# An attention and expert kernel: W1's transfers, the window copies, the early passes and the one-hots, re-cut

## The chip, the core and the metric

The kernel runs on one core of a Trainium2 chip. The metric is device time in microseconds of one execution; a median of three runs is given. PE is TensorE, DVE VectorE, ACT ScalarE, POOL GpSimd, SP SyncE, which here only issues transfers.

## What is computed

```python
# q, k, v: [8, 8, 576, 64] (batch, head, token, channel)
q_s = softmax(q, axis=-1); k_s = softmax(k, axis=2)
kv = einsum('bhsd,bhse->bhde', k_s, v)
x = einsum('bhsd,bhde->bhse', q_s, kv)         # as [4608, 512]
logits = x @ w_gate + modality_bias[modality_id]   # 8 experts
e_idx = argmax(logits); gate_w = softmax(logits)[e_idx]
for e in range(8):                              # w1 [512, 1024], w2 [1024, 512]
    out[mask] = gate_w * (relu(x[mask] @ w1[e]) @ w2[e])
```

There are two modalities. Each one's largest bias names the expert that the kernel assumes for its tokens; at the end it counts on the chip whether that held, and a loop (from line 1074) computes all experts if not.

## The kernel before, in words

Tokens are sorted by modality as they come out of the attention. `xs` holds 4,864 slots of x, transposed: tokens of modality a are filled in from the left, those of b from the right. For each batch, `attention(b)`:

- ACT takes the exponentials of q and k; DVE sums q's (line 642), and DVE or POOL multiplies by the inverse (`norm_q`, line 651, one instruction of 2,304 columns per batch). V is cast to bf16.
- PE forms kv (line 713), multiplies q by a 0/1 matrix that sorts each tile of 64 tokens (`perm`, made by nine comparisons in `perm_run`, line 675; PE line 780), ACT or DVE evicts (line 789), PE multiplies by kv (line 818).
- `put` (line 837) copies each of the nine tiles twice, to a's and to b's place: ACT writes a's, DVE writes b's. The place is a register; each batch loads nine of them on each of the two engines (`load_off`, line 758). A copy is 64 slots wide, and its last part may hold tokens of the other side, which the next copy of the same side overwrites; so copies of one side are chained.

`ffn` (line 952) runs passes over slots, `passes_a` and `passes_b` (line 203): start and width of the slots, and the batch after which they are full. In a pass PE computes 8 groups of h (line 934), ACT or DVE applies relu (lines 908, 910), PE computes y per 128 slots (line 944), the result is scaled by the gate (lines 914, 916), and POOL stores rows to their tokens by an indirect DMA (line 919). Before the first pass PE must have found which token stands in which slot: one-hots `hlo` and `hhi`, `hv` = `hhi` times the token numbers on POOL, and 36 matmuls (`id_run`, line 572). `hlo` lies in W's second half, so the second expert's casts wait for `id_run`.

The weights of the two experts come in eight tiles (`load_w`, line 414) through the same five fp32 buffers `st` as q, k and v, and are cast into `W`. A W1 tile is two transfers of 128 partitions whose pattern in DRAM is two blocks of 64 rows:

```python
ap=[[2 * Dh * F, 2], [F, Dh], [1, F]]
```

All of this is handed to a planner (`Plan.order`, line 83) as operations with costs per engine, dependencies, buffers and ranks. It plays them through and writes the program in the order in which it started them; transfers keep the order in which they were declared: q, k, v of batches 0 and 1, both experts' weights, then batches 2 to 7. On the chip each engine executes its list strictly in order.

## Time and profile before

| | |
|---|---|
| runs | 327.39 us median (327.07 to 327.65) |
| profiled execution | 328.85 us, span 327.1 us |
| busy in the span | PE 187.6, DVE 185.7, POOL 107.6, ACT 107.1 us |
| moved | 46.57 MB, 142 GB/s over the span |
| granted clock of PE | 0.893 mean |

Busy shares are averages over stages with different limits; they say little before the span is cut. Register and sequencer work is not in them. A wait is put down to what ended last.

### The profile page before, as it was taken

Reading aid. Unit: us, or ns where it says so; the run is one execution under the profiler, and the core shown is the slowest. Engines: PE = TensorE matmul, PEld = TensorE weight load, DVE = VectorE, ACT = ScalarE, POOL = GpSimd, SP = SyncE. Lnnn points to the kernel's source line nnn. Section 1 sums busy time; section 2 is a strip of 40 time slices with the busy share of each in tenths; the row PEclk is TensorE's granted clock in tenths of the full one; section 3 lists DMA queues with packets and bytes.
Section 4 is the critical chain, followed back from the end, with each engine's and each line's share of the span. In section 5 each row is a group of like instructions: output and inputs, shape, how many; then the busy total and the mean of one; then the engine's idle time right before and its main releaser. Section 6 shows DMA issues by size and latency. Waiting matters only on the chain. (4 is left out here: it accounts for less than half of the span.)

```text
span 327.1 us, 4307 instructions
## 1 busy us (share of the span) xinstructions
PE 187.6 (57%) x1450; PEld 107.1 (33%) x1471; DVE 185.7 (57%) x411; ACT 107.1 (33%) x192; POOL 107.6 (33%) x113
## 2 busy tenths in 40 slices
PE   0024400038600007679758966549879999999960
PEld 0023300026400005356424534225544444445520
DVE  1799670001700037649789959795776647567530
ACT  3227210035311017348696865525641000000000
POOL 5449000127100013536972629042201331413330
PEclk9999999999955555989979999598989999999995
DMA  7592114511114599897666981000200211202110
GB/s 257 162 395 110 54 53 125 188 52 51 55 53 150 171 362 308 282 355 262 256 213 206 395 325 64 2 0 34 97 3 24 105 65 65 116 33 111 57 54 25
DMA packets 20731, 46.57 MB, mean 142 GB/s; under 512 B 3039, under 2 KB 3039, under 8 KB 20704
## 3 DMA queue, kind: packets, MB, share of 16 engines
q1 hardware_dynamic: 15888, 36.70, 32.2%
q0 software_dynamic: 3040, 9.44, 7.4%
q10 hardware_dynamic: 1776, 0.10, 0.4%
q8 instruction: 13, 0.21, 0.3%
q14 instruction: 14, 0.11, 0.1%
HBM read 36.80 MB, written 9.96 MB: 143 GB/s over the span
## 5 line engine op out<-in xcount | busy, mean ns | idle before, releaser
L934 PE MATMUL ff<-xs,W 128*128 128x512 bf16 (+2 forms) x376 | 82.3, 371 | 43.6 <-ACT W L451 19.9
L944 PE MATMUL ff<-W,hT 128*128 128x512 bf16 x291 | 69.4, 386 | 1.1 <-issue 0.2
L919 POOL DMA_INDIRECT out_dram<-y_sb,idx x38 | 37.7, 992 | 95.9 <-DVE y_sb L916 67.6
L934 PEld LDWEIGHTS <-W 128*128 128x128 bf16 x384 | 39.7, 107 | 76.0 <-ACT W L451 21.8
L845 DVE CAST xs<-mm 128x256 f32 x72 | 30.6, 424 | 45.5 <-ACT xs L845 41.7
L944 PEld LDWEIGHTS <-hT 128*128 128x128 bf16 x304 | 29.5, 99 | 33.8 <-issue 1.9
L916 DVE TENSOR_SCALAR y_sb<-ff,gate 128x512 f32<-128x512 f32 x30 | 22.5, 749 | 26.4 <-PE ff L944 22.9
L910 DVE TENSOR_SCALAR hT<-ff 128x512 bf16<-128x512 f32 (+2 forms) x54 | 32.5, 605 | 7.7 <-PE ff L934 6.0
L845 ACT CAST xs<-mm 128x256 f32 (+1 forms) x72 | 27.3, 379 | 21.1 <-DVE xs L845 17.4
L453 POOL CAST W<-st 128x1024 bf16<-128x1024 f32 x7 | 7.3, 1040 | 78.5 <-DMA st<-in_moe_w_dram 39.1
L451 ACT CAST W<-st 128x1024 bf16<-128x1024 f32 x8 | 8.4, 1044 | 69.1 <-DMA st<-in_moe_w_dram 69.1
L652 POOL TENSOR_TENSOR eq<-st,qi 128x2304 bf16<-128x2304 f32 x5 | 20.2, 4048 | 21.7 <-DVE L L889 9.2
L678 POOL TENSOR_SCALAR perm<-iota_row,posx 128x128 bf16<-128x128 bf16 x36 | 23.3, 662 | 8.0 <-DVE posx L504 7.3
L878 PE MATMUL mm<-wg_sb,xs 128*128 128x8 bf16 x152 | 5.5, 168 | 31.2 <-DVE L L889 28.5
L818 PE MATMUL mm<-et,kvbd 128*128 128x128 bf16 (+1 forms) x160 | 14.3, 226 | 15.6 <-DVE xs L845 11.0
L639 ACT ACTIVATE st<-st 128x2304 f32<-128x2304 f32 x8 | 17.0, 2124 | 18.9 <-DMA st<-in_q_dram 16.8
L908 ACT ACTIVATE hT<-ff 128x256 bf16<-128x256 f32 (+1 forms) x42 | 19.3, 482 | 10.3 <-PE ff L934 6.0
L713 PE MATMUL kv<-vb,ek 64*128 64x129 bf16 x288 | 13.0, 246 | 16.8 <-DVE vb L668 16.4
L642 DVE TENSOR_REDUCE qi<-st 128x36 f32<-128x2304 f32 x8 | 20.3, 2542 | 2.4 <-issue 2.2
L780 PE MATMUL mm<-perm,eq 128*128 128x128 bf16 x144 | 14.5, 239 | 8.6 <-DVE eq L652 3.0
L818 PEld LDWEIGHTS <-kvbd 128*128 128x128 bf16 x160 | 11.4, 104 | 20.3 <-issue 16.7
L660 ACT ACTIVATE ek<-st 128x2304 bf16<-128x2304 f32 x8 | 17.0, 2122 | 2.4 <-DMA st<-in_k_dram 2.4
(106 smaller groups left out, 166.6 us busy)
## 6 DMA issues: line engine op xcount, KB each, us to landing
st<-in_q_dram SPq DMA_DIRECT2D x8, 1152.0 KB, 8.7
st<-in_k_dram SPq DMA_DIRECT2D x8, 1152.0 KB, 11.2
st<-in_v_dram SPq DMA_DIRECT2D x8, 1152.0 KB, 11.6
st<-in_moe_w_dram SPq DMA_DIRECT2D x16, 512.0 KB, 18.1
out_dram<-y_sb,idx POOLq DMA_INDIRECT x38, 2.7
mraw<-in_moe_modality_id_dram ACTq DMA_DIRECT2D x2, 36.0 KB, 8.6
wg_f<-in_moe_w_gate_dram ACTq DMA_DIRECT2D x4, 4.0 KB, 2.9
bias_b<-n_moe_modality_bias_dram ACTq DMA_DIRECT2D x1, 8.0 KB, 8.1
```

What stands on the lines that cost most here:

```text
L639: nc.scalar.activation(out=t, in_=t, func=ACT.Exp)
L642: nc.vector.tensor_reduce(out=small[qib.idx], in_=view(st[bq.idx], [[Dh, HG * NJ], [1, Dh]]), op=ALU.add, axis=AX.X)
L652: (nc.vector if e == "DVE" else nc.gpsimd).tensor_tensor(out=view(eq[eqb.idx], [[Dh, HG], [HG * Dh, NJ], [1, Dh]]), in0=view(st[bq.idx], [ ...
L678: (nc.vector if e == "DVE" else nc.gpsimd).tensor_scalar(out=perm[pmb.idx][:, j, :], in0=iota_row, scalar1=posx[:, c : c + 1], scalar2=Non ...
L818: nc.tensor.matmul(out=view(mm_t[xbuf.idx], [[1, nj * 64]], c * nj * 64), lhsT=kvbd[kvb.idx][:, c, :], rhs=et[etb.idx][:, c, j0 * 64 : (j0 ...
L845: w_ = nc.scalar.copy(out=dst, in_=src) if side == 0 else nc.vector.tensor_copy(out=dst, in_=src)
L908: nc.scalar.activation(out=dst, in_=src, func=ACT.Relu)
L910: nc.vector.tensor_scalar_max(out=dst, in0=src, scalar1=0.0)
L916: nc.vector.tensor_scalar(out=dst, in0=src, scalar1=g, scalar2=None, op0=ALU.mult)
L919: s_ = nc.gpsimd.indirect_dma_start(out=out, out_offset=bass.IndirectOffsetOnAxis(ap=ix[:, c : c + 1], axis=0), in_=ysb, in_offset=None, b ...
L934: nc.tensor.matmul(out=t[:, 0:w], lhsT=W[:, slot_, kd * F + f * P : kd * F + (f + 1) * P], rhs=xs[:, kd, lo : lo + w], start=(kd == 0), st ...
L944: nc.tensor.matmul(out=t, lhsT=h[:, kf, i * P : (i + 1) * P], rhs=W[:, slot_, W2 + kf * D : W2 + (kf + 1) * D], start=(kf == 0), stop=(kf ...
```

## The change

- W1: a tile comes as two transfers of 64 partitions, 2 x 1,024 values each, so that 64 rows are the outermost dimension on both sides. W2: a tile is one transfer instead of two. (The loop for all experts, which these inputs do not enter, is cut alike.)
- Window copies: both copies of a tile go to one engine, fixed per batch (`copier`): ACT in six batches, DVE in batches 2 and 5. That engine alone loads the offsets, nine instead of eighteen; b's place is computed from a's. Each copy is now made to follow the one two before it.
- Passes: per side 256, 256, 256, 256, 512, 512, 384 slots instead of 256, 256, 512, 512, 512, 384; slots 512 to 1,023 are due after batches 2 and 3 instead of 3.
- One-hots: `hlo` lies in the middle of `xs`, which no copy reaches before batch 3. The second expert's casts no longer wait for `id_run`; the clearing of the middle does, and so comes later. `hv` is made in six pieces. Offsets and the numbers compared are bf16.
- `norm_q` in five pieces; `perm` in one instruction on DVE, no longer on POOL. Ranks of casts and of the slot work are lower, that is earlier.

```diff
-    passes_a = [(0, 0, 256), (1, 256, 256), (3, 512, 512), (5, 1024, 512), (7, 1536, 512), (7, 2048, 384)]
+    passes_a = [(0, 0, 256), (1, 256, 256), (2, 512, 256), (3, 768, 256), (5, 1024, 512), (7, 1536, 512), (7, 2048, 384)]
...
-    hlo = view(W[:, 1, :], [[P, HC], [1, P]])
+    def hlo(c, n):
+        a = CAP - HC // 8 * P + (c % (HC // 4)) * P
+        return xs[:, c // (HC // 4), a : a + n * P].rearrange("p (c m) -> p c m", m=P) if n > 1 else xs[
+            :, c // (HC // 4), a : a + P
+        ]
...
+                if part < 2:
+                    for g in range(2):
                         nc.sync.dma_start(
-                            out=st[buf.idx][:, c * F : (c + 1) * F],
+                            out=view(t, [[F, 2], [1, F]], 0, (64 * g, 64)),
                             in_=bass.AP(
                                 tensor=moe_w1.tensor,
-                                offset=eids[eid] * (D * F) + (4 * hp + hl) * Dh * F,
-                                ap=[[2 * Dh * F, 2], [F, Dh], [1, F]],
+                                offset=eids[eid] * (D * F) + (2 * g + part) * Dh * F,
+                                ap=[[F, Dh], [4 * Dh * F, 2], [1, F]],
                             ),
                         )
...
-                deps = [ld] + ([o_id] if s == 1 else [])
                 casts.append(
                     pl.op(
-                        {**on_act(F), **on_dve(F, 2), **on_pool(F, 1.05)}, cast, deps, rank=40 + s, uses=[buf]
+                        {**on_act(F), **on_dve(F, 2), **on_pool(F, 1.05)}, cast, [ld], rank=5 + 10 * s, uses=[buf]
...
-    o_hv = pl.op(on_pool(HC * NSL * 2, 2.85), hv_run, [o_hhi], rank=30)
+    o_hv = [pl.op(on_pool(HC * NSL // 3, 2.57), hv_run(i), [o_hhi], rank=16) for i in range(6)]
+    c_mid = pl.op({"POOL": (1.9, 2.1)}, clear_mid, [o_id], rank=25)
...
+    copier = ["ACT", "ACT", "DVE", "ACT", "ACT", "DVE", "ACT", "ACT"]
...
-        def perm_run(e):
-            for j in range(NJ):
-                c = b * NJ + j
-                (nc.vector if e == "DVE" else nc.gpsimd).tensor_scalar(
-                    out=perm[pmb.idx][:, j, :],
-                    in0=iota_row,
-                    scalar1=posx[:, c : c + 1],
-                    scalar2=None,
-                    op0=ALU.is_equal,
-                )
+        def perm_run(_):
+            nc.vector.tensor_tensor(
+                out=perm[pmb.idx],
+                in0=view(iota_row, [[0, NJ], [1, P]]),
+                in1=view(posx, [[1, NJ], [0, P]], b * NJ),
+                op=ALU.is_equal,
+            )
...
-        lo_a = pl.op({"ACT": (0.3, 0.4)}, load_off, [o_off, o_ki], rank=R + 3)
-        lo_b = pl.op({"DVE": (0.3, 0.4)}, load_off, [o_off, o_ki], rank=R + 3)
+        lo = pl.op({copier[b]: (2.0, 2.1)}, load_off, [o_off, o_ki], rank=R + 3)
...
-                        w_ = nc.scalar.copy(out=dst, in_=src) if side == 0 else nc.vector.tensor_copy(out=dst, in_=src)
+                        w_ = nc.scalar.copy(out=dst, in_=src) if e == "ACT" else nc.vector.tensor_copy(out=dst, in_=src)
...
+                    before = win[-2] if len(win) > 1 else filled[b - 1][side - 2] if b else None
                     win.append(
                         pl.op(
-                            on_dve(256) if side else on_act(256),
+                            on_dve(256) if copier[b] == "DVE" else on_act(256),
                             put,
-                            [o3, c_mid, lo_b if side else lo_a],
+                            [o3, c_mid if b >= 3 else None, lo, before],
```

What this makes of the program's order, at three places. First SP's queue, after v of batch 1: the first expert's first tiles. Before (names are `st` buffers and the weights in DRAM; sizes are partitions and the dimensions in one):

```order
L323 DMA st1_64<-in_v_dram 128x4x576
L425 ISA
L425 DMA st2_65<-in_moe_w1_dram 128x1x1024
...
L425 DMA st0_63<-in_moe_w1_dram 128x1x1024
...
L435 DMA st4_67<-in_moe_w2_dram 128x2x512
...
L435 DMA st1_64<-in_moe_w2_dram 128x2x512
```

Now:

```order
L330 DMA st1_64<-in_v_dram 128x4x576
L431 ISA
L431 DMA st2_65<-in_moe_w1_dram 64x2x1024
...
L431 DMA st0_63<-in_moe_w1_dram 64x2x1024
...
L440 DMA st1_64<-in_moe_w2_dram 128x4x512
L440 ISA
L440 DMA st2_65<-in_moe_w2_dram 128x4x512
```

The order of the tiles is kept (each W1 row stands twice, for two transfers); W2's second tile now uses the buffer of W1's first.

Second ACT, from batch 1's last copies to the exponential of batch 2's q. Before (line 845 is a window copy, 451 a cast of W, 639 the exponential):

```order
L845 ISA
L845 COPY xs_61<-mm2_92 128x4x64
L451 CAST W_62<-st2_65 128x1024
L451 CAST W_62<-st0_63 128x1024
L451 CAST W_62<-st4_67 128x1024
L908 ACTIVATE hT1_81<-ff1_94 128x256
L895 ACTIVATE ex_143<-ex_143 128x16 x2
L451 CAST W_62<-st3_66 128x1024
L914 ACTIVATE y_sb0_82<-ff2_95,gate_145 128x512
L914 ACTIVATE y_sb1_83<-ff0_93,gate_145 128x512
L895 ACTIVATE ex_143<-ex_143 128x16 x2
L639 ACTIVATE st1_64<-st1_64 128x2304
```

Now (line 863 is a window copy, 456 a cast of W, 649 the exponential of q, 673 that of k):

```order
L673 ACTIVATE ek1_69<-st4_67 128x4x9x64
...
L456 CAST W_62<-st0_63 128x1024
L810 CAST et1_77<-mm2_92 128x4x128
L780 TENSOR_LOAD off_i_131
L810 CAST et1_77<-mm0_90 128x4x64
L456 CAST W_62<-st3_66 128x1024
L863 ISA
L863 COPY xs_61<-mm2_92 128x4x64
...
L863 COPY xs_61<-mm1_91 128x4x64
L649 ACTIVATE st2_65<-st2_65 128x2304
```

ACT's casts of the second expert's weights moved ahead of batch 1's copies, of which ACT now has 18 instead of 9; the exponential of k of batch 1 moved from ahead of batch 0's copies to behind them and behind relus.

Third PE, at the end of the last batch's attention. Before (line 818 is the last attention matmul, 934 a matmul of h):

```order
L818 MATMUL mm1_91<-et1_77,kvbd1_75 128x64
L934 LDWEIGHTS W_62
L934 MATMUL ff2_95<-xs_61,W_62 128x512
...
L934 MATMUL ff1_94<-xs_61,W_62 128x512
...
L878 LDWEIGHTS xs_61
L878 MATMUL mm2_92<-wg_sb_119,xs_61 128x8
```

Now (line 836 is the last attention matmul, 963 a matmul of y, 897 one of the logits):

```order
L836 MATMUL mm0_90<-et1_77,kvbd1_75 128x64
L963 LDWEIGHTS hT0_80
L963 MATMUL ff0_93<-W_62,hT0_80 128x512
...
L897 LDWEIGHTS xs_61
L897 MATMUL mm2_92<-wg_sb_119,xs_61 128x8
```

The first pass of 512 slots on side a is still in h there before the change, and in y after it.

## Rows read from the trace of the kernel before

**Rows 1.** The page's 40 equal slices: GB/s that DMA moved:

```profile
GB/s 257 162 395 110 54 53 125 188 52 51 55 53 150 171 362 308 282 355 262 256 213 206 395 325 64 2 0 34 97 3 24 105 65 65 116 33 111 57 54 25
```

**Rows 2.** Busy us: PE, PEld, DVE, ACT, POOL; clock, DMA share, GB/s:

```profile
26.00:126.50 100.50, 25.54 (x241) 17.77 (x241) 30.93 (x71) 24.16 (x52) 18.83 (x20) 0.82 0.36 123
126.50:241.50 115.00, 84.82 (x783) 50.89 (x793) 90.39 (x178) 71.07 (x129) 54.43 (x44) 0.91 0.53 188
241.50:316.10 74.60, 74.13 (x385) 35.54 (x393) 46.67 (x94) 2.47 (x7) 20.09 (x21) 0.98 0.17 64
316.10:327.10 11.00, 0.00 (x0) 0.00 (x0) 1.09 (x4) 0.00 (x0) 1.28 (x2) 0.61 0.14 53
```

**Rows 3.** The same view, stretches in which one kind of transfer runs:

```profile
14.00:26.00 12.00, 2.86 (x44) 2.59 (x44) 11.85 (x34) 3.83 (x2) 7.20 (x8) 1.00 1.02 387
28.00:52.00 24.00, 5.25 (x58) 4.01 (x58) 16.59 (x30) 5.98 (x13) 4.02 (x3) 1.00 0.13 53
66.00:100.00 34.00, 15.66 (x150) 10.81 (x152) 7.38 (x19) 11.19 (x25) 9.39 (x13) 0.85 0.13 53
```

**Rows 4.** SP's own queue in order of time: start us, us, what:

```profile
20.09 23.06 SPq L425 DMA_DIRECT2D st<-in_moe_w_dram  x4
...
62.34 29.23 SPq L425 DMA_DIRECT2D st<-in_moe_w_dram  x4
...
110.66 2.93 SPq L323 DMA_DIRECT2D st<-in_q_dram  x1
```

**Rows 5.** Who waited for whom: us in total, times, longest:

```profile
ACT W L451 <- DMA st<-in_moe_w_dram: 69.1, 8, 21.6
```

**Rows 6.** ACT in order of time:

```profile
21.28 2.12 ACT L639 ACTIVATE st<-st 128x2304 f32<-128x2304 f32 x1 [9.17 <-DMA st<-in_q_dram]
...
36.35 1.04 ACT L451 CAST W<-st 128x1024 bf16<-128x1024 f32 x1 [4.46 <-DMA st<-in_moe_w_dram]
...
126.51 2.12 ACT L639 ACTIVATE st<-st 128x2304 f32<-128x2304 f32 x1 [0.56 <-DMA st<-in_q_dram]
```

**Rows 7.** The chain of waits at the end: start us, us, what:

```profile
241.10 0.38 ACT xs L845
...
255.62 6.91 PE ff L934 x32
```

**Rows 8.** DMA issues: KB each, median us to landing:

```profile
st<-in_moe_w_dram SPq DMA_DIRECT2D x16, 512.0 KB, 18.1
```

**Rows 9.** ACT's and DVE's groups by shape: busy, mean ns of one, idle before:

```profile
L845 ACT CAST xs<-mm 128x256 f32 x71 | 26.9, 379 | 20.3 <-DVE xs L845 17.4 <-PE ff L944 1.2 <-PE mm L818 0.6
...
L908 ACT ACTIVATE hT<-ff 128x512 bf16<-128x512 f32 x19 | 10.9, 596 | 2.1 <-PE ff L934 2.0
L908 ACT ACTIVATE hT<-ff 128x256 bf16<-128x256 f32 x23 | 8.4, 388 | 8.2 <-PE ff L934 4.0 <-issue 2.5 <-PE mm L780 1.7
...
L845 DVE CAST xs<-mm 128x256 f32 x72 | 30.6, 424 | 45.5 <-ACT xs L845 41.7 <-PE ff L934 0.4
...
L548 DVE TENSOR_TENSOR W<-iota_row,lo 128x1152 bf16<-128x1152 bf16 x4 | 5.3, 1333 | 0.2 <-issue 0.2
```

**Rows 10.** The offset loads, line 761: ns min/median/max, first and last start:

```profile
L761 ACTq TENSOR_LOAD <-off_i x8: 778/1967/2687, 24.3 to 222.6; - x8
L761 DVEq TENSOR_LOAD <-off_i x8: 853/2082/2742, 25.6 to 222.9; - x8
```

**Rows 11.** POOL's and DVE's rows in order of time, two places:

```profile
170.15 4.05 POOL L652 TENSOR_TENSOR eq<-st,qi 128x2304 bf16<-128x2304 f32 x1 [1.20 <-DVE qi L649]
...
199.69 4.05 POOL L652 TENSOR_TENSOR eq<-st,qi 128x2304 bf16<-128x2304 f32 x1
...
170.83 3.42 DVE L891 TENSOR_TENSOR ex<-L,gmx 128x32 f32<-128x32 f32 x1
...
199.01 7.16 DVE L678 TENSOR_SCALAR perm<-iota_row,posx 128x128 bf16<-128x128 bf16 x9
...
219.25 1.52 DVE L678 TENSOR_SCALAR perm<-iota_row,posx 128x128 bf16<-128x128 bf16 x9
```

More of the change, by code (lines that the diff above doesn't have):

```diff
@@ L317 @@
     c_dve2 = pl.op({"DVE": (0.9, 1.1)}, consts_dve2, [c_pool], rank=-8)
-    c_mid = pl.op({"POOL": (2.3, 2.4)}, clear_mid, [c_pool], rank=-8)
     def load(src, b, buf):
@@ L576, in id_run @@
                 out=view(t, [[NSL, 2], [1, NSL]]),
-                lhsT=hlo[:, c, :],
+                lhsT=hlo(c, 1),
                 rhs=hv[:, c],
@@ L635, in attention @@
         qib, kib, kvp = Buf(r_qi), Buf(r_kinv), Buf(r_kv)
+        groups = [(j0, min(2, NJ - j0)) for j0 in range(0, NJ, 2)]
         def exp_q(_):
@@ L649, in inv_q, with norm_q, run @@
             nc.vector.reciprocal(out=t, in_=t)
-        def norm_q(e):
-            (nc.vector if e == "DVE" else nc.gpsimd).tensor_tensor(
-                out=view(eq[eqb.idx], [[Dh, HG], [HG * Dh, NJ], [1, Dh]]),
-                in0=view(st[bq.idx], [[NJ * Dh, HG], [Dh, NJ], [1, Dh]]),
-                in1=view(small[qib.idx], [[NJ, HG], [1, NJ], [0, Dh]]),
-                op=ALU.mult,
-            )
+        def norm_q(j0, n):
+            def run(e):
+                (nc.vector if e == "DVE" else nc.gpsimd).tensor_tensor(
+                    out=view(eq[eqb.idx], [[HG * Dh, n], [Dh, HG], [1, Dh]], j0 * HG * Dh),
+                    in0=view(st[bq.idx], [[Dh, n], [NJ * Dh, HG], [1, Dh]], j0 * Dh),
+                    in1=view(small[qib.idx], [[1, n], [NJ, HG], [0, Dh]], j0),
+                    op=ALU.mult,
+                )
+            return run
         def exp_k(_):
@@ L692, in attention @@
         iq = pl.op({"DVE": (0.35, 0.5)}, inv_q, [sq], rank=R + 1, uses=[qib])
-        nq = pl.op({**on_dve(S * HG), **(on_pool(S * HG, 2.8) if b > 1 else {})}, norm_q, [iq], rank=R + 1, takes=[eqb], uses=[qib, bq])
+        nq = []
+        for j0, n in groups:
+            n_ = n * HG * Dh
+            nq.append(
+                pl.op(
+                    {**on_dve(n_), **(on_pool(n_, 1.76) if b > 1 else {})},
+                    norm_q(j0, n),
+                    [iq] + nq[:1],
+                    rank=R + 1,
+                    takes=[] if nq else [eqb],
+                    uses=[eqb, qib, bq],
+                )
+            )
         vcost = on_dve(S * 2, 2) if b < 1 else {**on_pool(S * 2, 1.03), **on_dve(S * 2, 2)}
@@ L752, in attention @@
         o_kb = pl.op({"DVE": (0.7, 0.8)}, kvbd_run, [o_ki, c_dve], rank=R + 2, takes=[kvb], uses=[kvp, kib])
-        groups = [(j0, min(2, NJ - j0)) for j0 in range(0, NJ, 2)]
         ets, win, firsts = [], [], []
@@ L758, in load_off @@
         def load_off(e):
-            eng = ENG.Activation if e == "ACT" else ENG.DVE
-            side = 0 if e == "ACT" else 1
             vs = nc.values_load_multi_w_load_instructions(
-                off_i[0:1, side, b * NJ : (b + 1) * NJ],
-                engines=[eng],
+                off_i[0:1, b * NJ : (b + 1) * NJ],
+                engines=[ENG.Activation if e == "ACT" else ENG.DVE],
                 min_val=0,
-                max_val=NSLOT - 64,
+                max_val=N - 64,
                 skip_runtime_bounds_check_because=WHY,
             )[1]
-            av.append((side, vs))
-        lo_a = pl.op({"ACT": (0.3, 0.4)}, load_off, [o_off, o_ki], rank=R + 3)
-        lo_b = pl.op({"DVE": (0.3, 0.4)}, load_off, [o_off, o_ki], rank=R + 3)
+            av.extend(vs)
+        lo = pl.op({copier[b]: (2.0, 2.1)}, load_off, [o_off, o_ki], rank=R + 3)
         for gi, (j0, nj) in enumerate(groups):
@@ L844, in put @@
                         src = view(mm_t[xbuf.idx], [[nj * 64, KD], [1, 64]], jj * 64)
-                        w_ = nc.scalar.copy(out=dst, in_=src) if side == 0 else nc.vector.tensor_copy(out=dst, in_=src)
-                        if not started["ab"[side]]:
+                        w_ = nc.scalar.copy(out=dst, in_=src) if e == "ACT" else nc.vector.tensor_copy(out=dst, in_=src)
+                        if b >= 3 and not started["ab"[side]]:
                             started["ab"[side]] = True
@@ L1099 @@
                 hl, hp = part // 2, part % 2
-                nc.sync.dma_start(
-                    out=t[:, 0:F],
-                    in_=bass.AP(
-                        tensor=moe_w1.tensor,
-                        offset=e * (D * F) + (4 * hp + hl) * Dh * F,
-                        ap=[[2 * Dh * F, 2], [F, Dh], [1, F]],
-                    ),
-                )
+                for g in range(2):
+                    nc.sync.dma_start(
+                        out=t[64 * g : 64 * g + 64, 0:F],
+                        in_=bass.AP(
+                            tensor=moe_w1.tensor,
+                            offset=e * (D * F) + (4 * hp + 2 * g + hl) * Dh * F,
+                            ap=[[F, Dh], [1, F]],
+                        ),
+                    )
             else:
```

83 lines of the change are left out of this document (41 added, 42 removed).

## The prediction

> **What bounds the kernel now.** I read the page's slices first, then the busy time by stage, then DMA alone, then who waits. The slices show the hole: for about 90 us after the first eighth of the span the core moves some 50 GB/s in most slices, with one bump in the middle [rows 1]. By stage the same hole is 26 to 126.5 us: 100.5 us in which no engine is busy for more than 31 us [rows 2]. DMA alone says why. Between 14 and 26 us, when q, k and v arrive, the DMA share is 1.02 at 387 GB/s. In 28 to 52 and again in 66 to 100 us, when the first weight matrix of an expert (W1) arrives, it is 0.13 at 53 GB/s [rows 3]. 0.13 of sixteen engines is two engines, and W1's source pattern begins with a dimension of 2. The queue's own rows fit: each expert's four W1 issues hold SP for 23 and 29 us, so that q of batch 2 is issued only at 110.66 us [rows 4]. ACT waits 69.1 us for weights, more than anything else waits for anything [rows 5].
>
> After that there are two stages. From exp of q2 (126.51 us [rows 6]) to the last window copy (241.1 us to 241.5 [rows 7]) DVE is busy 90.4, PE 84.8 and ACT 71.1 of 115 us [rows 2]. From there only expert matmuls are left, PE is 99% busy for 74.6 us, and the last 11 us store rows and check [rows 2].
>
> So I cost the change in three terms: when q2 is exponentiated, how long the attention stage of batches 2 to 7 takes, what is left after it.
>
> **Term 1, the weights.** The 16 weight issues carry 512 KB each [rows 8], 8.39 MB, half of it W1. At 53 GB/s W1's 4.19 MB take 79 us. In the new form both patterns begin with 64, and half a tile goes to each half of the partitions. The trace has no large transfer with 64 outermost, so I bound it: 53 GB/s (outermost 2) and 387 GB/s (outermost 128) [rows 3]. I take 387: if the share follows the outermost count, 64 is above sixteen. W1 then takes 10.8 us, a saving of 68 us of queue time; all weights and q2 (8 x 576 x 64 values of 4 bytes, 1.18 MB) are 9.57 MB, 24.7 us. First q, k, v are in by 26 us [rows 3], so q2 could land at about 51 us plus the few us from issue to landing. W2's four issues per expert become two of 1 MB; the same bytes in the same queue, costed at nothing, since before they were delayed by W1 ahead of them.
>
> Landing is no longer what is late. ACT executes in program order, and in the new order it has, between exp of q1 at 21.28 us [rows 6] and exp of q2: the two exps (q1, k1) at 2.12, two offset loads at 1.97 [rows 10], 36 window copies at 0.40 (0.379 [rows 9] and the gap between chained copies), 8 evictions of about 0.6, 7 casts of W at 1.04 [rows 6], 8 relus at 0.388 [rows 9], and 1.1 of gates and scaling. That is 4.2 + 3.9 + 14.4 + 4.8 + 7.3 + 3.1 + 1.1 = 39 us, so exp of q2 not before 60 us. The casts wait for tiles whose buffers are freed in turn: W1's second tile needs q0's buffer, W2's second tile needs W1's first tile cast, expert 1's last tile needs k1's exp, which now stands behind casts and relus on ACT. I add 3 us and take **63 us**, with 71 us as the upper end if W1 arrives at half the rate, and 60 us as the lower. Against 126.5 us this is 63.5 us gained.
>
> [...] The trace shows full rate only for transfers that span 128 partitions [rows 3]. [...]
>
> **Term 2, batches 2 to 7.** Costs that leave DVE: 18 window copies of 0.424 (two of the six batches on DVE, where half of each was) = 7.6 us [rows 9]; four of six offset loads of 2.08 = 8.3 us [rows 10], which the busy time does not hold: sequencer time in which DVE stands still. perm becomes one instruction of 1152 columns instead of nine. The kernel has one of that size with two bf16 SBUF inputs, but inside a group with a float offset; I take 1.33 us, that row [rows 9], against 1.52 us for nine when undisturbed and 7.16 us when POOL normalizes q at the same time [rows 11]. Four of them now in this stage: 5.3 against 8.7. Similarly a gate subtraction took 3.42 us while POOL's normalization of 4.05 us ran [rows 11]. POOL's normalization is now in five pieces; if a piece takes its share of 4.05, DVE is held for at most 0.9 us at a time. Over this stage I count 5 us back for it; nothing to 8 are the ends. Costs that come: two more passes of 256 per side in place of one of 512, so 18 more gate instructions of some 0.18 (3.2), four more relus of 256 and three of 512 (3.5, a little over ACT's price [rows 9]); scaling and casts of v that go elsewhere -5. Normalization pieces +1. DVE stood at 90.4 + 6 x 2.08 = 103 of 115 us, 90%. It comes to 103 - 7.6 - 8.3 - 3.4 - 5 + 3.2 + 3.5 - 5 + 1 = 81 us.
>
> ACT takes over. It stood at 71.1 + 6 x 1.97 = 83 us [rows 2, 10]. It gains 18 copies (7.2), loses two loads (3.9), and by the order has 39 relus of 256 and 2 of 512 where it had 14 and 16 (+1.3), four more scalings (2.8), four more gate exps (0.9), one eviction less: 91 us. PE gains some 7 us of expert work, 92 us. So the fullest engines are PE and ACT, and this stage cannot be under 92 us. At the 90% that DVE reached it would be 102; at ACT's present share of 72% it would be 126. Three engines between 75% and 85% full are harder to interleave than one at 90%, so I take **108 us**, 7 less than now.
>
> The one-engine copies make the chain of a batch no shorter: 18 chained copies of 0.40 are 7.3 us on ACT, where they now run partly beside DVE's. hlo in xs in place of W's second half: W's second expert no longer waits for the index matmuls; this is inside term 1. Clearing the middle of xs now waits on POOL for the index matmuls; behind it there stand two casts of expert 1's W2 (1.04 each), which the second pass needs late, and batch 3's copies come tens of us after it: nothing. The product of the one-hots takes POOL as long in six pieces as in one, but lets casts and DVE's two-input operations in between: nothing, inside term 1's 3 us. The bf16 offsets and the fewer offset instructions are under 1 us: nothing.
>
> **Term 3, what is left.** In PE's order 116 matmuls of 512 columns for h and 176 for y follow the last attention matmul now; 92 and 160 in the changed kernel; those of 384 stay 64. Thirty-two take 6.91 us [rows 7], 0.216 each: 40 x 0.216 = 8.6 us less. From 241.0 to 327.1 is 86.1 us now, so **77.5 us**.
>
> **Sum.** 63 + 108 + 77.5 = 248.5 us of span. The profiled execution's own time, 328.85 us, is 1.75 above its span of 327.1, and the median of the runs, 327.39, is 1.46 below that execution; the median should be 249 us.
>
> **Rivals.**
> 1. Half rate. [...] For it: no row shows 64 partitions at full rate. Against its full price: ACT's 39 us hide part. Exp of q2 at 66 to 71; 252 to 257 us, say 255. [...] Chance 0.20.
> 2. ACT becomes the bound and is filled no better than now: stage 126 us, 267 us. For it: 72 of the 108 copies of this stage now stand in ACT's queue ahead of relus on which PE waits; PE already waits for relus and copies in this stage. Against: fewer handovers between ACT and DVE, which now cost ACT 17.4 us of waits [rows 9]. Chance 0.15.
> 3. The change doesn't do what it says: W1 stays at 53 GB/s, because the spread follows another dimension (the inner 2). Only terms 2 and 3 come, 7 + 8.6 = 15.6: 312 us. [...] Chance 0.03.
> 4. Slower: the 64-partition form lands on a single engine, 26.5 GB/s, half of what two give [rows 3]. W1 takes 158 us, 79 more, less 15.6: 391 us. It decides from where W1 takes longer than 79 + 15.6 us, that is under 44 GB/s; near that rate the kernel would be level (0.01). Against: 64 can be divided much more finely than 2. Chance 0.02.
>
> **How the numbers follow.** The forecast, 240 to 257 us, has 0.59. From the lower ends (60 + 98 + 77.5 = 235.5) to rival 2 (267) lie more than 8 in 10, so the range is 235 to 267. Faster by over 0.2%, about what a measurement here can tell from no change: 0.59 + 0.20 + 0.15 + 0.03 = 0.97; same 0.01; slower 0.02.
>
> **What would show it.** Step 1: DMA share near 1 and over 350 GB/s while W1 arrives (rival 1: near half; rival 3: 0.13), exp of q2 at 60 to 66 us, SP's issues under 1 us each. Step 2: DVE without 3 us subtractions, perm under 1.4 us, 102 to 115 us from exp of q2 to the last copy, with ACT the fuller engine (rival 2: over 120 with PE waiting on ACT's hT and xs). Step 3: 76 to 79 us from the last copy to the end. The prediction fails if W1's rate is under 150 GB/s, or if the stage of batches 2 to 7 leaves 92 to 126 us.

## The result and the profile after

The changed kernel takes 239.77 us, the median of four runs (235.93 to 242.71); the kernel before, on the same chip, 327.52 (327.07 to 327.69). The ratio is 0.7254, 95% interval 0.717 to 0.7339; it goes by the two faster of the four runs (239.16 and 235.93), the median by all four. The forecast was 249 (235 to 267): it lies inside, 9 us below the middle. The profiled execution took 240.39 us with a span of 238.6.

| term | predicted | profile after |
|---|---|---|
| exp of q2 starts | 63 us | 65.56 us |
| from there to the end of the last window copy | 108 us | 95.9 us |
| from there to the end | 77.5 us | 77.1 us |

Almost all of the miss is in the middle term. The stages, in the view of busy time by stretch (the columns are those of [rows 2]):

```profile
26.00:65.60 39.60, 23.57 (x227) 16.41 (x226) 34.03 (x51) 23.96 (x60) 24.81 (x18) 0.96 1.02 283
65.60:161.50 95.90, 85.52 (x888) 56.42 (x887) 81.82 (x172) 75.18 (x166) 50.58 (x48) 0.96 0.65 239
161.50:226.70 65.20, 65.20 (x369) 31.79 (x367) 42.01 (x87) 2.08 (x6) 19.04 (x20) 1.00 0.19 71
226.70:238.60 11.90, 0.03 (x2) 0.00 (x0) 1.10 (x4) 0.00 (x0) 1.30 (x2) 0.63 0.14 50
```

The first stage fell from 100.5 us to 39.6, and no hole is left in it: DMA's share is 1.02 where it was 0.36, and DVE is busy for 34.0 of the 39.6 us. In the second stage PE is now the fullest engine, 85.5 of 95.9 us, where DVE was [rows 2]. The third is 65.2 us of PE without a gap.

DMA alone, in the same view. The stretches answer to [rows 3]: q, k and v first; then W1; then W2 of the second expert and q2, k2, v2:

```profile
14.00:26.00 12.00, 4.98 (x57) 3.67 (x57) 11.84 (x40) 4.55 (x6) 0.00 (x0) 1.00 1.03 388
26.00:34.00 8.00, 2.81 (x24) 2.05 (x22) 7.97 (x7) 5.26 (x19) 3.69 (x2) 1.00 1.04 219
...
54.00:70.00 16.00, 12.76 (x115) 8.65 (x114) 10.27 (x33) 11.93 (x29) 7.28 (x6) 0.89 1.05 394
```

W1 comes at 219 GB/s with all sixteen engines busy (1.04). It was 53 GB/s with two of them (0.13). So the engines are spread now, and yet the rate is a little over half of the 388 that q, k and v reach. This is the half-rate rival's rate; what it goes with is tried below.

ACT in order of time, the rows that answer to [rows 6]:

```profile
20.73 2.12 ACT L649 ACTIVATE st<-st 128x2304 f32<-128x2304 f32 x1 [8.45 <-DMA st<-in_q_dram]
...
26.43 5.07 ACT L863 CAST xs<-mm 128x256 bf16<-128x256 f32 x18 [0.24 <-PE mm L836]
34.88 1.04 ACT L456 CAST W<-st 128x1024 bf16<-128x1024 f32 x1 [3.37 <-DMA st<-in_moe_w_dram]
39.18 1.99 ACT L456 CAST W<-st 128x1024 bf16<-128x1024 f32 x2 [3.26 <-DMA st<-in_moe_w_dram]
...
63.45 2.31 ACT L863 CAST xs<-mm 128x256 f32 x8
65.56 2.21 ACT L649 ACTIVATE st<-st 128x2304 f32<-128x2304 f32 x1
```

No wait stands before exp of q2 (before, it waited for q's transfer, [rows 6]): it runs when ACT's list comes to it. ACT's own work does not fill the time up to there, though: ACT is busy for 24.0 of the 39.6 us of this stage. What held the list up stands in the chain of work that ended last (start us, us, what):

```profile
25.78 13.38 DMA st<-in_moe_w_dram
...
44.34 10.52 DMA st<-in_moe_w_dram
...
55.99 1.82 POOL xs L321
57.86 0.33 PE mm L897 x7
```

Two transfers of W1 take 24 us of it. Behind the second, POOL casts a tile of W and then clears the middle of `xs` (line 321), and PE waits for that with its logits (line 897). Relus, ACT's copies and exp of q2 follow. ACT's wait for weights fell from 69.1 [rows 5] to 10.8 us:

```profile
ACT W L456 <- DMA st<-in_moe_w_dram: 10.8, 5, 3.4
```

And batch 0's eighteen copies take 5.07 us, 0.28 each. The sum had 0.40. The page's group says the opposite if it is read alone:

```profile
L863 ACT CAST xs<-mm 128x256 f32 (+1 forms) x108 | 32.2, 444 | 3.2 <-PE ff L953 2.1
```

A mean of 444 ns against 379 before [rows 9], so each copy seems dearer; 108 x 0.444 is 48 us, but the group was busy for 32.2. Copies of the two sides overlap: the mean is the time that one is in flight, the busy time is what the engine gives to them, 0.30 each here.

### The profile page after: what moved, and what is told of

It reads as the page before. It is cut to its first block, busy times and chain, and to the rows that moved or that the text cites. A ratio compares the mean times of both kernels' runs of the same rounds, so it can differ in the third digit from the quotient of the medians.

```text
span 238.6 us, 4394 instructions
## 1 busy us (share of the span) xinstructions
PE 179.6 (75%) x1535; PEld 108.6 (46%) x1535; DVE 175.5 (74%) x378; ACT 111.3 (47%) x238; POOL 98.2 (41%) x104
## 4 chain that ended last, share of the span: by engine, by line
PE 46%; DVE 20%; DMA 14%; ACT 8%; issue 5%; SPq 1%; POOL 1%; ACTq 0%; DVEq 0%; POOLq 0%
PE ff L963 22%; PE ff L953 18%; DMA st<-in_moe_w_dram 10%; DMA mraw<-in_moe_modality_id_dram 4%; DVE qi L652 3%; DVE xs L863 3%; DVE eq L663 2%; DVE perm L689 2%; ACT xs L863 2%; DVE ex L910 2%; PE mm L836 2%; ACT ek L673 2%; PE mm L798 1%; ACT et L810 1%; SPq L431 1%
## 5 line engine op out<-in xcount | busy, mean ns | idle before, releaser
L953 PE MATMUL ff<-xs,W 128*128 128x256 bf16 (+2 forms) x448 | 78.4, 323 | 6.3 <-DVE hT L929 3.9
L953 PEld LDWEIGHTS <-W 128*128 128x128 bf16 x448 | 43.3, 101 | 31.3 <-issue 6.8
L963 PEld LDWEIGHTS <-hT 128*128 128x128 bf16 x304 | 29.3, 99 | 32.2 <-issue 1.6
L929 DVE TENSOR_SCALAR hT<-ff 128x512 bf16<-128x512 f32 (+2 forms) x62 | 35.7, 580 | 6.8 <-PE ff L953 5.1
L863 ACT CAST xs<-mm 128x256 f32 (+1 forms) x108 | 32.2, 444 | 3.2 <-PE ff L953 2.1
L681 POOL CAST vb<-st 128x1152 bf16<-128x1152 f32 x10 | 13.4, 1349 | 38.4 <-DMA st<-in_v_dram 38.4
L663 POOL TENSOR_TENSOR eq<-st,qi 128x512 bf16<-128x512 f32 (+1 forms) x24 | 25.1, 1072 | 7.4 <-DVE kinv L760 4.7
L798 PEld LDWEIGHTS <-eq 128*128 128x128 bf16 x144 | 11.0, 107 | 18.6 <-DVE eq L663 12.9
L810 ACT CAST et<-mm 128x512 bf16<-128x512 f32 (+1 forms) x30 | 15.2, 536 | 3.2 <-PE mm L798 1.7
L663 DVE TENSOR_TENSOR eq<-st,qi 128x512 bf16<-128x512 f32 (+1 forms) x16 | 15.8, 1027 | 0.0
L735 PEld LDWEIGHTS <-ek 64*128 64x128 bf16 x288 | 9.3, 99 | 11.9 <-issue 7.9
## 6 DMA issues: line engine op xcount, KB each, us to landing
st<-in_moe_w_dram SPq DMA_DIRECT2D x4, 1024.0 KB, 12.1
```

What stands on the lines that cost most here:

```text
L663: (nc.vector if e == "DVE" else nc.gpsimd).tensor_tensor(out=view(eq[eqb.idx], [[HG * Dh, n], [Dh, HG], [1, Dh]], j0 * HG * Dh), in0=view( ...
L735: nc.tensor.matmul(out=kv_t[:, hg, 130 * hp : 130 * hp + 129], lhsT=ek[ekb.idx][rows, j, P * hp : P * hp + P], rhs=vb[vbb.idx][rows, j, hp ...
L798: nc.tensor.matmul(out=view(t, [[2 * nj * 64, 2], [1, 64]], hp * nj * 64 + jj * 64), lhsT=eq[eqb.idx][:, j0 + jj, P * hp : P * hp + P], rh ...
L863: w_ = nc.scalar.copy(out=dst, in_=src) if e == "ACT" else nc.vector.tensor_copy(out=dst, in_=src)
L929: nc.vector.tensor_scalar_max(out=dst, in0=src, scalar1=0.0)
L953: nc.tensor.matmul(out=t[:, 0:w], lhsT=W[:, slot_, kd * F + f * P : kd * F + (f + 1) * P], rhs=xs[:, kd, lo : lo + w], start=(kd == 0), st ...
```

## The experiments

Each was timed beside the kernel before. To separate the stages I read in each profile the start of exp of q2, the end of the last window copy and the end.

| kernel | median us (runs) | exp of q2 | to last copy | to the end |
|---|---|---|---|---|
| changed | 239.77 (235.93 to 242.71) | 65.56 | 95.9 | 77.1 |
| changed, again | 240.12 (239.24 to 240.51) | 63.67 | 96.8 | 77.0 |
| before + W1's form | 267.34 (265.94 to 268.60) | 64.98 | 115.8 | 85.7 |
| W1's old form | 302.68 (302.15 to 303.48) | 127.66 | 96.4 | 76.4 |
| two queues | 243.05 (240.68 to 244.84) | 68.59 | 93.1 | 77.3 |
| 16 partitions each | 245.68 (243.34 to 248.77) | 67.45 | 97.1 | 77.1 |
| W1 in 128 rows (another output) | 237.78 (236.81 to 238.20) | 63.78 | 95.2 | 76.8 |
| chained copies | 248.68 (245.20 to 249.79) | 65.28 | 103.9 | 77.2 |
| norm and perm as before | 246.34 (245.69 to 247.67) | 66.36 | 108.3 | 71.3 |
| passes as before | 239.72 (237.47 to 240.46) | 66.46 | 90.5 | 81.6 |
| copies on both engines | 260.82 (258.13 to 261.42) | 63.41 | 118.4 | 74.5 |
| q2 first | 241.69 (238.50 to 242.30) | 46.91 | 113.8 | 79.8 |
| hv on DVE | 246.13 (244.74 to 248.80) | 66.81 | 96.9 | 79.3 |

The second row is the changed kernel once more, timed beside "copies on both engines" and "q2 first":

> The changed kernel once more, unchanged, on the same chip as the two beside it, for its own spread: 236 to 243 us, median 239 to 240.

Its ratio to before is 0.7329 (0.7305 to 0.7353). The two profiles of one kernel differ by 1.9 us at exp of q2: less than that is not read out of a single profile here.

### W1's form alone

```diff
-                            out=st[buf.idx][:, c * F : (c + 1) * F],
+                            out=view(st[buf.idx], [[F, 2], [1, F]], 0, (64 * c, 64)),
...
-                                offset=eids[eid] * (D * F) + (4 * hp + hl) * Dh * F,
-                                ap=[[2 * Dh * F, 2], [F, Dh], [1, F]],
+                                offset=eids[eid] * (D * F) + (2 * c + part) * Dh * F,
+                                ap=[[F, Dh], [4 * Dh * F, 2], [1, F]],
```

> The kernel before with W1's two transfers per tile cut into 64 partitions each, and nothing else. Theory: W1's transfers are the whole of term 1, and terms 2 and 3 need the other edits. W1 arrives at 216 to 226 GB/s as in the changed kernel, 4.19 MB in 19 us in place of 79, exp of q2 at 66 to 72 us instead of 126.5, the stage behind it 115 us and the tail 86 us as before: about 270 us (262 to 278). Rival: the earlier ranks of the casts and the one-hots' new home were needed for it too (the second expert's casts wait for the index matmuls, and the buffers of its tiles with them): exp of q2 at 80 us or later, 283 us or more.

267.34 us, ratio 0.8139 (0.8092 to 0.8185). Exp of q2 at 64.98, as early as with the whole change; W1 at 218 GB/s:

```profile
26.00:34.00 8.00, 3.22 (x27) 2.57 (x25) 7.89 (x14) 5.24 (x13) 6.18 (x3) 1.00 1.04 218
65.00:180.80 115.80, 87.25 (x786) 52.39 (x797) 92.32 (x178) 71.11 (x130) 54.36 (x44) 0.89 0.53 197
```

The stage behind is as long as before, 115.8 us against 115 [rows 2], with DVE again the fullest. So the four lines on W1 are all of term 1. The earlier casts and the one-hots' new home were not needed for it.

### Everything but W1's form

```diff
-                            out=view(t, [[F, 2], [1, F]], 0, (64 * g, 64)),
+                            out=t[:, c * F : (c + 1) * F],
...
-                                ap=[[F, Dh], [4 * Dh * F, 2], [1, F]],
+                                ap=[[2 * Dh * F, 2], [F, Dh], [1, F]],
```

> The changed kernel with W1 in the old transfers of 128 partitions (outermost dimension 2). Theory: W1 at 53 GB/s again, 79 us of queue, exp of q2 at 118 to 127 us, and behind it the changed kernel's 96 and 77 us: 292 to 300 us, say 297. Rival (as recorded in the prediction): the stage of batches 2 to 7 is as I costed it, 108 us, and only 15.6 us come: 312 us.

302.68 us, ratio 0.9234 (0.9201 to 0.9267), between two theories, 2.7 us above the first one's upper end. Exp of q2 comes at 127.66 and the two stages behind are the changed kernel's (96.4 and 76.4 us). W1 alone gives 328.27 - 267.34 = 60.9 us, everything else alone 328.27 - 302.68 = 25.6: together 86.5, and the whole change 87.8. The two halves of the change add up.

### Why half the rate

Two kernels put the halves of a tile in flight together. First one half from SP, the other from POOL:

```diff
-                        nc.sync.dma_start(
+                        (nc.sync, nc.gpsimd)[g].dma_start(
```

> The changed kernel with the two halves of a W1 tile on two queues: partitions 0 to 63 from SP, 64 to 127 from POOL, so that both halves are in flight at once. [...] Then W1 goes at 300 to 390 GB/s while both are in flight, ACT's 10.4 us of waits for W's tiles shrink, and the end comes 4 to 9 us earlier: 231 to 236 us. Rival: the rate belongs to the form of the transfer (64 rows, two pieces of 4 KB each, two blocks apart), whoever issues it: 216 to 226 GB/s again and 238 to 242 us, or later if POOL's issues stand behind its other work.

243.05 us, ratio 0.7427 (0.7368 to 0.7486): no gain, the rival. That two halves in flight would add up their rates was my estimate; no row had shown it. Then eight transfers of 16 partitions, lower and upper half in turn:

```diff
+                    for r in range(0, Dh, 16):
                         for g in range(2):
...
-                            out=view(t, [[F, 2], [1, F]], 0, (64 * g, 64)),
+                            out=view(t, [[F, 2], [1, F]], 0, (64 * g + r, 16)),
...
-                                ap=[[F, Dh], [4 * Dh * F, 2], [1, F]],
+                                ap=[[F, 16], [4 * Dh * F, 2], [1, F]],
```

> The changed kernel with a W1 tile in eight transfers of 16 partitions that alternate between the lower and the upper half, all from SP. [...] If each engine finishes one transfer before the next, or if the form of the pieces limits, the rate stays at 216 to 226 and the time at 238 to 242; if the number of transfers counts (64 in place of 16 for W1), the issues hold SP longer and it is slower than 242.

245.68 us, ratio 0.752 (0.7466 to 0.7575): slower than the changed kernel. Neither shows yet whether the partitions or the 4 KB pieces are at fault, so one transfer of 128 partitions with the same pieces. What this kernel leaves out is the pairing of W1's rows with x's channels: the rows stand at other partitions, so its output is another one. It moves the same bytes and does the same amount of work:

```diff
-                    for g in range(2):
...
-                            out=view(t, [[F, 2], [1, F]], 0, (64 * g, 64)),
+                        out=view(t, [[F, 2], [1, F]]),
...
-                                offset=eids[eid] * (D * F) + (2 * g + part) * Dh * F,
-                                ap=[[F, Dh], [4 * Dh * F, 2], [1, F]],
+                            offset=eids[eid] * (D * F) + part * 2 * P * F,
+                            ap=[[F, P], [P * F, 2], [1, F]],
```

> The changed kernel with a W1 tile in one transfer of 128 partitions, 128 rows in a row of memory outermost, the same 4 KB pieces and the same bytes (the rows of W1 then stand at other partitions than x's channels, so h is computed with the rows of W1 in another order). It tells apart why the two-queue run had both halves in flight at only 218 to 256 GB/s. Theory: the span of partitions limits; W1 then goes at 380 GB/s or more, ACT's 10.4 us of waits for W fall to a few, exp of q2 at 57 to 62 us in place of 65.6, time 231 to 237 us. Rival: pieces of 4 KB limit (300 ns each in the changed kernel, against 84 ns for W2's 2 KB); then W1 stays at 216 to 226 GB/s and the time at 238 to 242 us.

Here are the three in the view by stretch, each while W1 alone arrives. Two queues, both halves in flight:

```profile
44.00:48.00 4.00, 4.00 (x21) 2.82 (x20) 3.96 (x4) 2.86 (x6) 2.44 (x3) 1.00 1.02 241
```

16 partitions each:

```profile
30.00:36.00 6.00, 1.02 (x8) 0.69 (x8) 5.96 (x7) 1.45 (x6) 1.85 (x2) 1.00 1.04 163
```

128 rows in one transfer:

```profile
26.00:30.00 4.00, 2.30 (x20) 1.81 (x19) 4.00 (x2) 3.76 (x16) 2.34 (x2) 1.00 1.03 409
```

The same bytes in the same pieces go at 409 GB/s when one transfer spans 128 partitions, at 219 when it spans 64, at 163 when it spans 16. The DMA share is full in all three, so the engines are busy but each piece takes longer: by the packets' own times, a 4 KB piece of W1 took 159 ns in the first case and 307 in the second (medians). Between 128 and 64 partitions it is not the 4 KB pieces, then: the rate goes with the span of one transfer. Why a piece takes longer no run shows. The transfers of 16 partitions are also smaller, 128 KB in place of 512, and the two were not separated. A second transfer to the other half beside the first adds 10% (241 against 219, from one stretch of 4 us; those from 42 and from 46 us, which overlap it, show 230 and 241), not 100%. So the half-rate rival had the rate right, and it is not that one half waits for the other.

What is full rate worth? This kernel's time is 237.78 us, ratio 0.7228 (0.7197 to 0.7259) against 0.7329 (0.7305 to 0.7353) of the changed kernel's second series: about 1%; against the first series (0.7254, 0.717 to 0.7339) no difference shows. Its exp of q2 starts at 63.78 us, as in the second profile of the changed kernel. W1 delays ACT less there, and PE delays it more: between 26 us and exp of q2 ACT waits 2.4 us for W in place of 10.8, and 8.7 for PE in place of 3.0, of which 5.0 for batch 1's attention. DVE is full:

```profile
26.00:63.78 37.78, 22.59 (x226) 16.92 (x225) 37.16 (x51) 23.87 (x60) 26.75 (x18) 0.95 0.93 344
```

I found no order of W1's rows that has this form and keeps the pairing, since x's channels of one chunk come from heads two apart.

### The copies' cadence

```diff
+                        for last in chain[-1:]:
+                            tc.add_manual_dep(
+                                w_.ins,
+                                last.ins.name,
...
+                        chain.append(w_)
```

> The changed kernel with each window copy made to wait for the copy just before it, so that copies of the two sides no longer overlap; the order of the program stays. Theory: the mis-sized step of term 2 is the price of a copy (0.28 us on ACT and 0.33 on DVE in place of 0.40 and 0.43). With the chain the cadence is 0.40 and 0.43 again, 72 x 0.12 + 36 x 0.10 = 12 us of engine time come back, and the stage from exp of q2 to the last copy takes 104 to 108 us in place of 95.9: 247 to 252 us. Rival: ACT had slack (78% busy in the stage), the copies hide, and the stage stays at 95 to 98 us: 239 to 242 us.

248.68 us; every run (245.20 to 249.79) is above every run of the changed kernel's second series (239.24 to 240.51). The stage from exp of q2 to the last copy takes 103.9 us in place of 95.9, the two other stages are the same to 0.3 us (against the second profile: 96.8 us, and exp of q2 1.6 us earlier there). ACT's rows of the same five and nine copies, chained:

```profile
104.32 2.08 ACT L864 CAST xs<-mm 128x256 f32 x5
...
106.86 3.64 ACT L864 CAST xs<-mm 128x256 f32 x9
```

and in the changed kernel:

```profile
103.03 1.52 ACT L863 CAST xs<-mm 128x256 f32 x5
...
104.92 2.69 ACT L863 CAST xs<-mm 128x256 f32 x9
```

0.40 to 0.42 us per copy against 0.30. The theory holds, in the stage just below its range of 104 to 108 us: 8.0 of the 12.1 us that term 2 was too long (7.1 of 11.2 by the second profile) are the overlap of copies that do not depend on their neighbour. The last batch's eighteen copies, chained and in the changed kernel:

```profile
161.94 7.26 ACT L864 CAST xs<-mm 128x256 f32 x18 [0.62 <-PE mm L837]
```

```profile
156.38 5.07 ACT L863 CAST xs<-mm 128x256 f32 x18 [0.62 <-PE mm L836]
```

In the kernel before they took 7.0 us on two engines, from this row to the last copy's end at 241.48 us [rows 7]:

```profile
234.44 0.38 ACT L845 CAST xs<-mm 128x256 f32 x1
```

### Copies on both engines

```diff
-        lo = pl.op({copier[b]: (2.0, 2.1)}, load_off, [o_off, o_ki], rank=R + 3)
+        lo = [pl.op({e: (2.0, 2.1)}, load_off, [o_off, o_ki], rank=R + 3) for e in ("ACT", "DVE")]
...
-                            on_dve(256) if copier[b] == "DVE" else on_act(256),
+                            on_dve(256) if side else on_act(256),
```

> The changed kernel with the copies given out as before: a's copy on ACT, b's on DVE in every batch, and both engines load the nine offsets. Theory: DVE takes 18 more copies and four more offset loads in batches 2 to 7 (14 us by the prediction's terms), ACT loses 18 copies and gains two loads; what remains is the price, since neighbouring copies of one side on one engine are chained again (0.38 to 0.43 us). Stage from exp of q2 to the last copy 103 to 110 us in place of 95.9, time 247 to 254 us. Rival: the sides on two engines run beside each other, so a batch's copies take no longer, and DVE has room: 239 to 243 us.

260.82 us, ratio 0.7968 (0.7937 to 0.7999): 20.7 us over the changed kernel's second series, more than the theory's 7 to 14. The stage takes 118.4 us. Eighteen copies and four offset loads come to DVE in this stage, 7.6 and 8.3 us by the prediction's prices. The waits tell of more (us in total, times, longest; of these, 5.5 and 10.9 us lie in the stage):

```profile
DVE xs L863 <- ACT xs L863: 16.1, 16, 5.9
```

```profile
ACT xs L863 <- DVE xs L863: 11.8, 19, 1.9
```

In the changed kernel there is no such wait. Before, [rows 9] has 41.7 and 17.4 us of them over the whole span, but 32.7 of the 41.7 are one wait in the hole. From 126 to 241 us there are

```profile
ACT xs L845 <- DVE xs L845: 14.9, 13, 6.3
...
DVE xs L845 <- ACT xs L845: 5.2, 9, 0.9
```

As these rows show it, two engines that fill `xs` in turn hold each other up: the last batch's eighteen copies take 7.6 us here (174.2 to 181.8), against 5.07. What makes them wait was not tried.

### Normalization and perm as before

```diff
+            for j in range(NJ):
+                (nc.vector if e == "DVE" else nc.gpsimd).tensor_scalar(
+                    out=perm[pmb.idx][:, j, :],
...
-        for j0, n in groups:
-            n_ = n * HG * Dh
...
+        nq = [pl.op({**on_dve(S * HG), **(on_pool(S * HG, 2.8) if b > 1 else {})}, norm_q, [iq], rank=R + 1, takes=[eqb], uses=[qib, bq])] * len(groups)
```

> The changed kernel with perm in nine comparisons (DVE or POOL) and norm_q in one piece, as before. Theory: POOL's long normalization holds DVE's two-input operations (3.4 us subtractions, 7 us perm), 5 to 8 us of DVE, and PE's first matmul of a batch waits for the whole normalization: stage 102 to 106 us in place of 95.9, 246 to 250 us. Rival: with the copies off DVE there is room for it: 239 to 243 us.

246.34 us, ratio 0.7484 (0.7459 to 0.751): 6.2 us over the second series. The stage to the last copy is 12.4 us longer and the tail 5.8 us shorter. Long holds are back, one of 3.61 and one of 3.07 us. POOL's normalization and DVE's subtractions in the groups by shape (mean ns after the bar):

```profile
L662 POOL TENSOR_TENSOR eq<-st,qi 128x2304 bf16<-128x2304 f32 x3 | 12.2, 4062 | 1.9 <-DVE kinv L748 1.9
...
L898 DVE TENSOR_TENSOR ex<-L,gmx 128x32 f32<-128x32 f32 x4 | 4.2, 1047 | 0.1
```

and in the changed kernel:

```profile
L663 POOL TENSOR_TENSOR eq<-st,qi 128x512 bf16<-128x512 f32 x18 | 21.6, 1222 | 7.4 <-DVE kinv L760 4.7 <-ACT xs L863 1.5 <-PE ff L953 0.6
...
L910 DVE TENSOR_TENSOR ex<-L,gmx 128x32 f32<-128x32 f32 x4 | 1.7, 415 | 0.1
```

The mean of four is the one hold of 3.61 us; the subtractions of 16 columns are slower in the changed kernel (777 ns on average, 542 here). So the holds are shorter there, but not gone: a piece holds POOL for 1.22 us, not the 0.9 that I worked out from 4.05, and single subtractions still take up to 2.08 us (2.72 in the second profile). Most of the gain in time is elsewhere in the stage than in these few rows; whether it is perm on POOL, DVE's share or PE's start on a batch's first piece was not separated.

### Passes as before

```diff
-    passes_a = [(0, 0, 256), (1, 256, 256), (2, 512, 256), (3, 768, 256), (5, 1024, 512), (7, 1536, 512), (7, 2048, 384)]
+    passes_a = [(0, 0, 256), (1, 256, 256), (3, 512, 512), (5, 1024, 512), (7, 1536, 512), (7, 2048, 384)]
```

> The changed kernel with the passes of before (slots 512 to 1023 in one pass of 512 per side, due after batch 3). Theory: some 40 matmuls of 512 columns of expert work go back behind the last attention matmul, so the tail from the last copy to the end is 85 to 87 us in place of 77.2, while the stage before it loses as much PE work, of which it gives back at most half since PE waits there anyway: 244 to 249 us. Rival: PE is what fills that stage (85.5 of 95.9 us), it shortens by what it loses, and the time is the same, 239 to 242 us.

239.72 us, ratio 0.7268 (0.7221 to 0.7314): the rival, no difference. The tail takes 4.5 us more, the stage ahead of it 5.4 less:

```profile
66.50:157.00 90.50, 79.76 (x800) 49.09 (x799) 82.13 (x161) 71.71 (x147) 45.26 (x43) 0.92 0.69 246
157.00:227.00 70.00, 70.00 (x391) 34.03 (x390) 45.48 (x91) 2.17 (x6) 19.72 (x21) 1.00 0.18 68
```

PE is busy for 79.8 + 70.0 = 149.8 of 160.5 us; in the changed kernel for 85.5 + 65.2 = 150.7 of 161.1. The edit moves PE's work from one stage to the other, and the end stays.

### Two tries to beat it

```diff
-    casts = [load_w(0, 0), load_w(1, 1)]
-    for b in range(2, B):
+    casts = [load_w(0, 0)]
+    load_batch(2)
+    casts.append(load_w(1, 1))
+    for b in range(3, B):
```

> The changed kernel with q, k and v of batch 2 declared, and so fetched, ahead of the second expert's weights. In the changed kernel DMA is full from 14 to 100 us and PE is idle for 36.8 of the first 65.6 us and for 10.4 of the 161 us behind, so what comes earlier for PE counts. Theory: exp of q2 at 48 to 56 us in place of 65.6, ahead of batch 1's copies in ACT's order; PE gets batch 2's attention 10 us earlier but the second expert's passes later; half of it stays: 230 to 236 us. Rival: the second expert's matmuls are what filled PE there, DMA's bytes are the same, and ACT's queue of 39 us is only reordered: 238 to 242 us.

241.69 us, ratio 0.7327 (0.7282 to 0.7371): the rival. Exp of q2 comes 16.8 us earlier than in the second series, and nothing follows from it:

```profile
26.00:49.00 23.00, 10.83 (x99) 7.40 (x98) 22.87 (x18) 16.40 (x33) 16.17 (x11) 1.00 1.03 301
49.00:65.00 16.00, 11.80 (x134) 8.24 (x133) 14.88 (x34) 7.99 (x22) 7.33 (x5) 0.79 1.04 286
65.00:161.00 96.00, 84.12 (x867) 57.44 (x868) 86.79 (x177) 73.46 (x171) 45.26 (x42) 0.98 0.65 234
```

From 26 to 65 us PE is busy for 22.6 us, where the changed kernel had 23.6 in nearly the same stretch. By this sum the second expert's matmuls went back as batch 2's came forward. DVE is what is full there, 22.87 of the first 23 us. Part of that is POOL: while it makes hv (34.6 to 43.8 us in the changed kernel's second profile), four pieces of the normalization take 5.23 us on DVE, which took 2.20 for batch 0. So hv on DVE:

```diff
-            nc.gpsimd.tensor_tensor(
+            nc.vector.tensor_tensor(
                 out=hv[:, i * n : (i + 1) * n],
```

> The changed kernel with the product of the one-hots (hv, six pieces) on DVE instead of POOL. While POOL makes it, 34.6 to 43.8 us, DVE's two-input instructions take longer: four pieces of batch 1's normalization 5.23 us against 2.20 for batch 0's, four of hlo 8.25 against 5.3 (1.33 each). Theory: POOL and DVE hold each other up there, so hv on DVE costs 3 us and gives back 6, batch 1's attention is 3 us or more earlier, and with it the copies that stand ahead of exp of q2: exp of q2 at 60 to 63 us against 63.7 to 65.6, time 234 to 238 us against 240. Rival: exp of q2 waits for the weights' arrival (ACT's casts) and DMA is full until 100 us; PE's work decides behind; then 239 to 242 us, as with batch 2's loads first.

246.13 us, ratio 0.7523 (0.7494 to 0.7552): slower, a miss for both. DVE, already the fullest engine of this stage, got 4.4 us more to do. In DVE's rows in order of time the four pieces still take almost 1 us each, with POOL's product gone:

```profile
33.70 3.90 DVE L663 TENSOR_TENSOR eq<-st,qi 128x512 bf16<-128x512 f32 x4
37.52 2.25 DVE L568 TENSOR_TENSOR hv<-hhi,vals 128x456 bf16<-128x456 bf16 x4
```

and the new order gives ACT a cast that it waits 7.6 us for:

```profile
39.04 1.04 ACT L456 CAST W<-st 128x1024 bf16<-128x1024 f32 x1 [7.59 <-DMA st<-in_moe_w_dram]
```

One operation's other home changed the planner's whole early order; what of the 6 us is the order and what the instruction was not separated. None of the versions that compute the same output beats the changed kernel.

## Why the prediction was right, and where it was not

**What bounds it: right.** W1's two engines were the hole; the form of its transfers alone is worth 60.9 of 87.8 us.

**Term 1: the time right, by errors that cancel.** I took 387 GB/s for W1 from the outermost dimension of 64; it is 219, and the half-rate rival had the rate right. But the time of exp of q2, 65.56 and 63.67 in two profiles, is as near to my 63 as to that rival's 66 to 71, and with full rate it is 63.78: the rate is worth about 1% of the whole. ACT's 39 us of work, on which I built the term, are not what sets this point: ACT is busy for 24.0 of 39.6 us. Inside the sum the 36 copies were too dear (18 take 5.07 us, not 7.2) and the waits for weights too cheap (10.8 us, not the 3 that I added). In the changed kernel W1's transfers and the clearing of the middle stand on the chain to exp of q2; at full rate DVE does, busy for 37.2 of 37.8 us, and DVE stands nowhere in my term. That both come to 64 us, and my sum to 63, is luck.

**Term 2: the step that failed is the price of a copy, 0.40 us ("0.379 [rows 9] and the gap between chained copies")** and 0.424 on DVE. Those rows were of copies that waited for the one before; in the changed kernel each follows the one two before, and they start 0.26 to 0.28 us apart when nothing else holds them. The chained run puts 7 to 8 us of the 11 to 12 back. The same price is under "The one-engine copies make the chain of a batch no shorter": at 0.40 that holds, 7.26 us chained on one engine against 7.0 before on two, but the changed kernel's eighteen take 5.07. Undoing the one-engine copies costs 20.7 us, more than any other edit but W1's; DVE's copies and loads, as I had counted them, are 15.9 us of DVE's time; the rest I had not counted. ACT did not take over either: with four offset loads of 1.97 us it comes to 75.2 + 7.9 = 83 us, where I had 91; DVE with two of 2.08 to 81.8 + 4.2 = 86, where I had 81. The remaining 4 us: I had 92 us of PE's work in this stage, and it was 85.5. PE's granted clock was 0.96 over the stage where it had been 0.91 [rows 2]; that this accounts for the rest is argued, not shown.

**Normalization and perm: about right.** I counted 5 us back for the holds and 3.4 for perm; undoing both costs 6.2 us of time; in its profile the stage is 12.4 us longer and the tail 5.8 shorter. The 0.9 us that a piece can hold DVE was too small: single subtractions took up to 2.08 us.

**Term 3: the number right, its meaning wrong.** 77.1 us against 77.5. But the 8.6 us that I booked as a gain of the passes are in the tail only: with the old passes the tail is 81.6, so 4.5 us of it are theirs and the rest came with the other edits, and the time is the same, since PE is 94% busy from exp of q2 to its last matmul (150.7 of 161.1 us). In [rows 2] it was 159.0 of 189.6. What was gained is idle time of PE, 30.6 to 10.4 us, and 8 us of PE's own time. That it can come out in term 2 or 3 and counts once, my sum did not see; it was right in total because I had also booked those 7 us as work that comes to PE in term 2.

**Costed at nothing.** The clearing of the middle behind the index matmuls was not free: PE's logits wait 3.2 us for it, as the waits of the changed kernel say. I had looked at batch 3's copies behind it and not at the logits. It stands on the chain to exp of q2 in both profiles of the changed kernel; no run takes it away, so what it costs in time stays open.

```profile
PE mm L897 <- POOL xs L321: 3.2, 1, 3.2
```

**Rivals.** ACT as the bound: no. Counted with its loads, as the 72% were, it is filled to 87% (83 of 95.9 us), and PE and DVE are fuller. W1 still at 53 GB/s, or on one engine: no.

## What to carry to other kernels

A DMA has two dimensions to look at. In these runs the outermost one goes with how many engines share it (a share of 0.13 of sixteen with 2, 1.04 with 64), and the span of partitions with how long each of their pieces takes (159 or 307 ns for 4 KB, 409 or 219 GB/s); read the DMA share and the GB/s side by side, since either alone hides one of them. A duration read off a chain is not a price: before it goes into a sum, see whether the instruction waited for its neighbour and whether it still will (a copy: 0.40 us chained, 0.30 not), and take busy time over count, not the mean of one (0.30 against 0.44 here). That an engine's list reaches a point without a wait does not say that its own work set the time: look at how busy it was on the way (ACT: 24.0 of 39.6 us), and at the chain. Where one engine is as full to the end as PE here (94%), sum its idle time over the whole remainder instead of stage by stage: moving its work about, or feeding it earlier in one place, changed the stages here and not the end (239.72 and 241.69 us against 240.12).
